# Pooled attention and two MoE layers on one core: down products without GpSimd, keys and values one unit ahead, weight units moved, tables in the weights' buffers

## Chip, cores and metric

One core of a Trainium2 chip runs the whole program in one launch. The metric is device time in microseconds (us). All matrix products are float32 in three passes: an operand is split into a rounded high part and the remainder, and high x high, high x low and low x high are added up in PSUM.

## What is computed

The reference, cut to what matters (q and k are drawn 8 times larger than here; the weights arrive as float64):

```python
B, H, S, D, pool = 8, 8, 576, 64, 8
k_p = k.reshape(B, H, S // pool, pool, D).mean(axis=3)      # the same for v_p
attn = softmax(q @ k_p.transpose(0, 1, 3, 2) / sqrt(D))
x = (attn @ v_p).transpose(0, 2, 1, 3).reshape(4608, 512)
h = x @ w_in                                                # 512 x 2048
y = (h * clip(h + 3, 0, 6) / 6) @ w_out                     # 2048 x 512
g = y @ w_gate                                              # 512 x 1536, w_val too
out = (g * sigmoid(g) * (y @ w_val)) @ w_out2               # 1536 x 512
```

## The kernel before

The program has four stretches.

**Start-up** computes the attention of the first 512 tokens. `load_first` stages its inputs in buffers that the weights will use later.

**The first stage** goes over nine blocks `j` of 512 tokens, and in each over 16 products `f` (`up`, 12 matmuls of 512 columns each, into one of three PSUM banks `h`). `act1` turns the result into `g` (ScalarE `t`, VectorE `g`, one of three `g32` buffers), and `store_g` writes it to `g_d` in HBM. Between the products stand, at two places per `f` (`attn_slot`), the steps of the attention for block `j + 1`. They are cut into units (a head pair and up to 256 queries); the table `when` (line 907) gives each step a unit offset and a place in the unit, and a sort over all units sets the order on every engine. `RK` sums keys on GpSimd, `K` transposes them and fills `kbd`; `S` scores, `X` exponents, `N`, `M` (GpSimd) normalise, `E` splits the tail, `T` transposes, `U` and `L` copy to `aT`, `V` multiplies with the values, `W` and `Y` write `x`. `R0` and `R1` sum values on GpSimd, `R` splits them into `vst` and `vtl`. Behind each product `prep_slot` does a step of a weight unit: the layers after the first product use sums and differences of weight quarters (Strassen-Winograd: 7 products in place of 8), and 26 units compute these tables and store them in HBM. A unit fetches (SyncE), rescales (ScalarE), joins the two halves of each float64 (VectorE, lines 127 and 130), sums (GpSimd, `sums_a` or `sums_b`), casts (ScalarE, 249), subtracts (VectorE, 252) and stores. 14 units (`PREP_A`) fall into the first stage. Block 8, the last, has no attention beside it. There `g` is stored from ScalarE's queue, four quarters of block 0's `g` (`gq`) are loaded at its start, and the seven tables `pw` of `w_out` at its end, when the first stage's pools close.

**The down stage** takes the nine blocks again, seven products each (`DN`; `down_b`, 48 matmuls of 256 columns in four chunks). The products' left sides are the quarters 11, 22, 12 or the sums S3 = 11 - 21, S2 = 22 - S3, S1 = S2 + 11, S4 = 12 - S2, computed in place in `gq`, each in two halves: S3 and S2 on VectorE, S1 and S4 on GpSimd (`sum_b`, line 803). `split_b` splits a chunk one product ahead into one of four `gb` buffers (ScalarE cast, line 135; VectorE subtraction, line 136). `evac_b` adds the results (line 841). The other 12 weight units run here, their sums on GpSimd.

**The second MoE** makes six passes over 768 tokens with seven-product schemes for all its products; its weight tables come through a ring of four tiles (`load_next`).

The order on each engine is the program's own (`manual_schedule`): an instruction that waits holds back all behind it on its engine, DMA issues on their queue too.

Of the kernel before, what the change touches and what calls it, by code (L numbers as in the profile page):

```python
# [23 lines left out]
def kernel(  # L24
# [45 lines left out]
    l1, l1_ps = ExitStack(), ExitStack()  # L70
    wu_p = l1.enter_context(tc.tile_pool(name="wu", bufs=F1))
    x_p = l1.enter_context(tc.tile_pool(name="x", bufs=2))
    t_p = l1.enter_context(tc.tile_pool(name="t", bufs=2))
# [9 lines left out]
    half = const.tile([P, 1], F32, name="half")  # L83

# [53 lines left out]
    class Weights:  # L138
# [14 lines left out]
        def convert(self):  # L153

            done, self.joined = self.joined, []
            parts = []
            for f, t in done:
                w = wu[f] = wu_p.tile([P, 2, KT, P], F32R, tag="wu", name="wu")
                w = w.rearrange("p a k f -> p a (k f)")
                nc.scalar.copy(out=w[:, 0], in_=f32(t))  # L160
                parts.append((w, t))
            scaled, self.scaled = self.scaled, []
            for f, s in scaled:
                t = t_p.tile([P, WC], I32, tag="w32", name="w32")
                join(s, t)
                self.joined.append((f, t))
            for w, t in parts:
                nc.vector.tensor_tensor(out=w[:, 1], in0=f32(t), in1=f32(w[:, 0]), op=ALU.subtract)
# [45 lines left out]
    def prep_step(u, step):  # L214
# [25 lines left out]
        elif step == 3:  # L240
            q = prep_t["f", u]
            if kind == "up":
                sums_a(nc.gpsimd, lambda n: q[:, A7[n]])
            else:
                sums_b(nc.gpsimd, lambda n: q[:, B7[n]])
# [18 lines left out]
    def x_tile(j):  # L264
        if j not in x_t:
            x_t[j] = x_p.tile([P, KT, 2, N], F32R, tag="x", name="x")
# [43 lines left out]
    def load_first(seg_n):  # L310
        def stage(name):
            return wu_p.tile([P, 2, POOL, D], F32, tag="wu", name=name)

        ks = [stage("ks") for _ in range(KT)]
        es_t.append(stage("es").rearrange("p h o d -> p (h o d)"))
        qs, vs, vt = ([stage(nm) for _ in range(KT // 2)] for nm in ("qs", "vs", "vt"))
# [258 lines left out]
    def act1(pool, ps):  # L575
        t = pool.tile([P, N], F32, tag="t", name="t")
        nc.scalar.activation(out=t, in_=ps, func=ACTF.Relu, bias=half, scale=1.0 / 6.0)  # L577
        g = pool.tile([P, N], F32, tag="g32", name="g32", bufs=3)
# [3 lines left out]
    def store_g(j, f, g, eng):  # L582
        eng.dma_start(out=g_d[j][:, :, f // NP1, f % NP1], in_=g.rearrange("p (r n) -> p r n", r=2))
# [204 lines left out]
    def load_pw(what):  # L788
        nc.sync.dma_start(
            out=f32(lb["pw", what]).rearrange("p f a n -> p (f a n)"),  # L790
            in_=s_w1[:, B7[what]].rearrange("p f a n -> p (f a n)"),
        )

    SLOT = {"11": 0, "S1": 0, "12": 1, "S4": 1, "21": 2, "S3": 2, "22": 3, "S2": 3}

    def sum_b(eng, j, what):
        a, b, op = {
            "S3": ("11", "21", ALU.subtract), "S2": ("22", "S3", ALU.subtract),
            "S1": ("S2", "11", ALU.add), "S4": ("12", "S2", ALU.subtract),
        }[what]  # L800
        for c in range(0, NP1, NP1 // 2):
            v = lambda x: gq[j, SLOT[x]][:, c:c + NP1 // 2]
            eng.tensor_tensor(out=v(what), in0=v(a), in1=v(b), op=op)  # L803

    def split_b(i, c):

        j, n = divmod(i, 7)
        if j < NB:
            t = gb[i, c] = lb["gb"].tile([P, 2, CB, MB], F32R, tag="gb", name="gb")
# [62 lines left out]
    for j in range(NB):  # L872
# [176 lines left out]
    right_b, left_b = ExitStack(), ExitStack()  # L1049
    with tc.manual_schedule():  # L1050
# [50 lines left out]
        pool, late = t_p, []  # L1101
        for j in range(NB):
            for f in range(F1):
                if j == NB - 1 and f == 0:
                    attn_ctx.close()
                    last_a = ExitStack()
                    lb["gq"] = right_b.enter_context(
                        tc.tile_pool(name="gq", bufs=1, side="right", reuse_waits="tile"))
                    pool = last_a.enter_context(
                        tc.tile_pool(name="tl", bufs=2, side="right", reuse_waits="tile"))  # L1110
                    for slot in (0, 3, 2, 1):
# [3 lines left out]
                if (j, f) == (NB - 1, F1 - 1):  # L1115
                    l1.close()
                    for nm, bufs in (("pw", 1), ("gb", 4)):
                        lb[nm] = left_b.enter_context(
                            tc.tile_pool(name=nm + "b", bufs=bufs, reuse_waits="tile"))
                    order = [what for _, _, what in DN]  # L1120
                    for n in (2, 3, 4, 1, 5, 0, 6):
                        what = order[n]
                        lb["pw", what] = lb["pw"].tile([P, NP1, 2, 2 * P], F32R, tag="pw" + what, name="pw")
                    for what in order:
                        load_pw(what)
                    for c in range(NCB):
                        split_b(0, c)
                attn_slot(j, 2 * f)
                g = act1(pool, hp)
                attn_slot(j, 2 * f + 1)  # L1130
                if j < NB - 1:
                    store_g(j, f, g, nc.sync)
                else:
                    for args in late:
                        store_g(*args, nc.scalar)
                    late = [(j, f, g)]
# [4 lines left out]
        for args in late:  # L1141
            store_g(*args, nc.scalar)
        last_a.close()
# [3 lines left out]

        for i in range(7 * NB):
            j, n = divmod(i, 7)
            if n == 0:  # L1150
                sum_b(nc.vector, j, "S3")
            down_b(i)
            if n == 1:
                sum_b(nc.vector, j, "S2")
            for c in range(NCB):
                split_b(i + 1, c)
            if n == 1:
                sum_b(nc.gpsimd, j, "S1")
                sum_b(nc.gpsimd, j, "S4")
            if 2 <= n <= 5:  # L1160
                load_g(j + 1, {2: 3, 3: 0, 4: 2, 5: 1}[n])
            evac_b(j, n)
            prep_slot(F1 * (NB - 1) + i)
            if j == NB - 1 and n >= 5:
                if n == 5:
# [4 lines left out]
                    l2["x"] = ctx.enter_context(  # L1170
                        tc.tile_pool(name="xc", bufs=1, side="right", reuse_waits="tile"))
                    l2["ys"] = ctx.enter_context(
                        tc.tile_pool(name="ys", bufs=1, side="right", reuse_waits="tile"))
                    load_y(0)
                for step in ((0, 1, 2), (3, 4, 5, 6))[n - 5]:
# [65 lines left out]
```

## Time and profile before

| what | us |
|---|---|
| median of 3 runs | 1958.4 (1957.16 to 1961.93) |
| profiled execution | 1956.7 |
| its span, first to last instruction | 1955.0 |
| TensorE busy in it | 1788.7 (91%) |
| VectorE busy | 1390.3 (71%) |
| ScalarE busy | 763.7 (39%) |
| GpSimd busy | 778.7 (40%) |

The profile names engines PE (TensorE), PEld (its weight loads), DVE (VectorE), ACT (ScalarE), POOL (GpSimd) and SP (SyncE). Busy time alone does not say what limits a stretch: an instruction that is held up inside counts as busy, and TensorE's busy time counts the same whether its clock is at the full or the lower level. PEclk is the mean granted clock as a share of the full one.

### The profile page before, as it was taken

How to read it: one execution, taken by the hardware profiler on the slowest of the kernel's cores; microseconds unless marked ns; L12 is line 12 of the kernel's file. 1: busy time of each engine (PE TensorE's matmuls, PEld its weight loads, DVE VectorE, ACT ScalarE, POOL GpSimd, SP SyncE). 2: the span in 40 equal slices, each digit the busy share in tenths (PEclk: the TensorE clock that was granted, in tenths of full speed). 3: DMA queues.
4: the chain of work that ended last, by engine and by line, in shares of the span. 5: the costliest groups of instructions: out<-in, count | busy, mean ns of one | idle time of the engine just before them, and what ended most of it. 6: DMA issues, size and time to landing. Idle time of an engine off the chain costs nothing.

```text
span 1955.0 us, 31356 instructions
## 1 busy us (share of the span) xinstructions
PE 1788.7 (91%) x11241; PEld 1669.5 (85%) x11241; DVE 1390.3 (71%) x2356; ACT 763.7 (39%) x1689; POOL 778.7 (40%) x886
## 2 busy tenths in 40 slices
PE   5998898888889988988889889999999999999999
PEld 3776686666767777888889889999999999999999
DVE  7766676666667368888888856766866767678566
ACT  5644444444434334544444432422422323224123
POOL 5336446365362024343433315335155053252360
PEclk8999999898989998999999899999999999999999
DMA  7745566465555785565555558797787887887876
GB/s 172 191 121 173 168 208 194 147 192 174 165 150 171 253 336 178 195 230 208 177 198 186 182 204 284 238 313 260 253 314 241 286 287 242 291 284 249 284 241 211
DMA packets 234828, 432.52 MB, mean 221 GB/s; under 512 B 86576, under 2 KB 168496, under 8 KB 218416
## 3 DMA queue, kind: packets, MB, share of 16 engines
q1 hardware_dynamic: 228176, 425.00, 65.6%
q10 hardware_dynamic: 6496, 5.51, 0.8%
q8 instruction: 89, 1.46, 0.3%
q14 instruction: 67, 0.55, 0.1%
HBM read 326.11 MB, written 104.33 MB: 220 GB/s over the span
## 4 chain that ended last, share of the span: by engine, by line
PE 45%; DVE 3%; issue 1%; DMA 1%; POOL 0%; ACT 0%; SPq 0%; ACTq 0%; DVEq 0%
PE b L648 41%; PE b L825 4%; DVE gb L136 2%; DVE gq L803 0%; DMA sdn<-s 0%; DVE s L252 0%; DMA ystg<-y 0%; POOL q L195 0%; DVE o L841 0%; DVE xc L136 0%; ACT gb L135 0%; DVE ystg L195 0%; POOL gq L803 0%; DVE q L127 0%; ACT xc L135 0%
## 5 line engine op out<-in xcount | busy, mean ns | idle before, releaser
L648 PE MATMUL b<-xc,wr 128*128 128x384 f32 x3024 | 527.8, 336 | 7.6 <-ACT xc L135 5.9
L648 PEld LDWEIGHTS b<-xc,wr 128*128 128x128 f32 x3024 | 525.5, 188 | 8.7 <-ACT xc L135 6.2
L566 PE MATMUL h<-x,wu 128*128 128x512 f32 x1728 | 456.5, 418 | 1.6 <-DVE g L579 1.6
L825 PE MATMUL b<-gb,pw 128*128 128x256 f32 x3024 | 393.1, 294 | 54.6 <-DVE gb L136 43.1
L825 PEld LDWEIGHTS b<-gb,pw 128*128 128x128 f32 x3024 | 385.2, 201 | 62.6 <-DVE gb L136 50.4
L566 PEld LDWEIGHTS h<-x,wu 128*128 128x128 f32 x1728 | 339.5, 202 | 73.2 <-DVE g L579 2.0
L657 DVE TENSOR_TENSOR c<-c,b 128x384 f32<-128x384 f32 x504 | 265.1, 552 | 178.0 <-PE b L648 154.3
L695 POOL TENSOR_TENSOR s<-s,c 128x384 f32<-128x384 f32 x144 | 143.1, 1019 | 411.0 <-ACT s L693 411.0
L136 DVE TENSOR_TENSOR gb<-gq,gb 128x512 fp32r<-128x512 f32 x252 | 247.5, 1020 | 72.8 <-ACT gb L135 72.2
L648 PE MATMUL b<-wr,gc 128*128 128x256 f32 x2268 | 273.1, 283 | 0.0
L648 PEld LDWEIGHTS b<-wr,gc 128*128 128x128 f32 x2268 | 272.9, 189 | 0.0
L135 ACT CAST gb<-gq 128x512 fp32r<-128x512 f32 x252 | 154.5, 621 | 221.7 <-PE b L825 199.0
L702 POOL TENSOR_TENSOR gf<-s,c 128x384 f32<-128x384 f32 x144 | 168.7, 1197 | 66.4 <-DVE c L657 65.9
L135 ACT CAST gc<-gf 128x768 fp32r<-128x768 f32 x126 | 105.7, 839 | 192.3 <-POOL gf L702 101.0
L803 POOL TENSOR_TENSOR gq<-gq 128x1024 f32<-128x1024 f32 x36 | 109.7, 3067 | 175.1 <-DVE gq L803 134.3
L501 POOL TENSOR_TENSOR e<-e,sm 96x288 f32<-96x288 f32 (+3 forms) x85 | 61.0, 717 | 252.5 <-DVE sm L497 195.8
L579 DVE SCALAR_TENSOR_TENSOR g<-t,h 128x512 f32<-128x512 f32 x144 | 98.2, 683 | 85.3 <-ACT t L577 64.3
L693 ACT ACTIVATE s<-c 128x384 f32<-128x384 f32 x144 | 73.4, 525 | 203.6 <-DVE c L657 202.4
L136 DVE TENSOR_TENSOR gc<-gf,gc 128x768 fp32r<-128x768 f32 x126 | 133.8, 1093 | 17.4 <-ACT gc L135 15.8
L577 ACT ACTIVATE t<-h,half 128x512 f32<-128x512 f32 x144 | 98.3, 682 | 41.8 <-PE h L566 33.3
L665 ACT COPY c<-b 128x384 f32<-128x384 f32 x72 | 33.9, 470 | 146.1 <-PE b L648 146.1
L458 PE MATMUL pss<-kbd,qT 128*128 128x144 f32 (+2 forms) x336 | 62.5, 305 | 22.5 <-ACT kbd L404 20.5
(105 smaller groups left out, 1758.1 us busy)
## 6 DMA issues: line engine op xcount, KB each, us to landing
wr<-sup SPq DMA_DIRECT2D x72, 1024.0 KB
wr<-sdn SPq DMA_DIRECT2D x84, 768.0 KB
wr<-sup SPq DMA_DIRECT2D x72, 768.0 KB
gq<-g SPq DMA_DIRECT2D x36, 1024.0 KB
g<-g SPq DMA_DIRECT2D x128, 256.0 KB
sup<-s SPq DMA_DIRECT2D x12, 1792.0 KB
wstg<-in_moe_w_out_dram SPq DMA_DIRECT2D x56, 256.0 KB
sw<-s SPq DMA_DIRECT2D x8, 1792.0 KB
```

The source lines that it names most:

```text
L135: nc.scalar.copy(out=hi, in_=src)
L136: lo_engine.tensor_tensor(out=lo, in0=src, in1=f32(hi), op=ALU.subtract)
L566: nc.tensor.matmul(out=ps, lhsT=w(kt, wh), rhs=x(kt, xh), start=first and n == 0, stop=last and n == 3 * len(kts) - 1,)
L577: nc.scalar.activation(out=t, in_=ps, func=ACTF.Relu, bias=half, scale=1.0 / 6.0)
L579: nc.vector.scalar_tensor_tensor(out=g, in0=t, scalar=1.0, in1=ps, op0=ALU.min, op1=ALU.mult)
L648: nc.tensor.matmul(out=ps, lhsT=w(wh), rhs=x(xh), start=first and n == 0, stop=last and n == 2)
L657: add = lambda dst, a, b: nc.vector.tensor_tensor(out=dst, in0=a, in1=b, op=ALU.add)
L693: nc.scalar.activation(out=g[q], in_=c[q], func=ACTF.Sigmoid)
L695: nc.gpsimd.tensor_tensor(out=g[q], in0=g[q], in1=c[q], op=ALU.mult)
L702: nc.gpsimd.tensor_tensor(out=gf[p][:, GP[TURN[q]], f], in0=g[q], in1=c[q], op=ALU.mult)
L803: eng.tensor_tensor(out=v(what), in0=v(a), in1=v(b), op=op)
L825: nc.tensor.matmul(out=ps[:, d], lhsT=w[:, CB * c + k, wh, P * d:P * (d + 1)], rhs=g[:, gh, k], start=what == place and (c, d, k, m) == (0 ...
```

## The change

- **Down stage.** S1 and S4 run on VectorE, in halves laid out over products 1 to 5. S3 is gone from this stage: `act1` computes it on GpSimd in the first stage, in place in `g`, before the store, for the products `f` < 8. The remaining weight units are summed on VectorE. The quarters of the next block are loaded behind products 3, 4 and 5 in place of 2 to 5.
- **Attention order.** `RK`, `K`, `R0`, `R1`, `R` move one unit ahead; `V`, `W`, `Y` move eight places later in their unit.
- **Weight units.** 20 in the first stage, one every 5.5 products in place of 8; six in the down stage, one every nine.
- **Buffers.** The weights of four `f` share one 4096-column buffer of four; `load_first` takes slices of the same. The tables `pw` go into a buffer of their own (the first), the two `x` buffers and the weights' four, each as block 8's last product has read it. `g` is stored from SyncE's queue in all blocks, and has three `t` buffers.
- **Second MoE.** The ring lies elsewhere, and its first load is issued two products earlier.

```diff
-    PREP_A = 14
+    PREP_A = 20
     for u in range(len(preps)):
-        first = 8 * u if u < PREP_A else F1 * (NB - 1) + 9 * (u - PREP_A) // 2
+        first = 11 * u // 2 if u < PREP_A else F1 * (NB - 1) + 9 * (u - PREP_A)
...
-            q = prep_t["f", u]
+            q, eng = prep_t["f", u], nc.gpsimd if u < PREP_A else nc.vector
             if kind == "up":
-                sums_a(nc.gpsimd, lambda n: q[:, A7[n]])
+                sums_a(eng, lambda n: q[:, A7[n]])
...
+        if f < NP1:
+            nc.gpsimd.tensor_tensor(out=g[:, MB:], in0=g[:, :MB], in1=g[:, MB:], op=ALU.subtract)
         return g
...
-        "RK": (-1, 14), "K": (0, 11), "P": (-1, 4), "S": (1, 0), "X": (1, 1), "N": (1, 5),
-        "M": (1, 5), "E": (1, 12), "T": (2, 16), "U": (2, 17), "L": (2, 18), "V": (3, 6),
-        "W": (3, 7), "Y": (3, 12), "R0": (1, 21), "R1": (2, 15), "R": (2, 19),
+        "RK": (-2, 14), "K": (-1, 11), "P": (-1, 4), "S": (1, 0), "X": (1, 1), "N": (1, 5),
+        "M": (1, 5), "E": (1, 12), "T": (2, 16), "U": (2, 17), "L": (2, 18), "V": (3, 14),
+        "W": (3, 15), "Y": (3, 20), "R0": (0, 21), "R1": (1, 15), "R": (1, 19),
...
+                    load_g(0, 0)
+                    load_pw(0, lambda name: lb["px"].tile([P, BIG], F32R, tag="px", name=name))
+                    load_pw(1, big_x)
+                    for slot in (3, 2, 1):
                         load_g(0, slot)
...
+                store_g(j, f, g)
...
+                if j == NB - 1:
+                    if f % 4 == 3:
+                        load_pw(2 + f // 4, big_w)
+                    if 10 <= f < 10 + NCB:
+                        split_b(0, f - 10)
...
+        sums_at = {1: (("S2", 0), ("S2", 1)), 2: ((), ("S1", 0)), 3: (("S1", 1), ()),
+                   4: ((), ("S4", 0)), 5: (("S4", 1), ())}
...
-            if n == 0:
-                sum_b(nc.vector, j, "S3")
             down_b(i)
-            if n == 1:
-                sum_b(nc.vector, j, "S2")
             for c in range(NCB):
+                if c % (NCB // 2) == 0 and sums_at.get(n, ((), ()))[c // (NCB // 2)]:
+                    sum_b(j, *sums_at[n][c // (NCB // 2)])
                 split_b(i + 1, c)
-            if n == 1:
-                sum_b(nc.gpsimd, j, "S1")
-                sum_b(nc.gpsimd, j, "S4")
-            if 2 <= n <= 5:
-                load_g(j + 1, {2: 3, 3: 0, 4: 2, 5: 1}[n])
+            for slot in {3: (0,), 4: (2,), 5: (3, 1)}.get(n, ()):
+                load_g(j + 1, slot)
```

Three places of the engines' order. The first is VectorE in the down stage, from the last `g` to the adds of products 2 and 5 of block 0 (`gb<-gq,gb` is the subtraction of a split, `gq<-gq` half a sum, `o` an evacuation add). Before:

```order
L803 TENSOR_TENSOR gq<-gq 128x1024 x2
L136 TENSOR_TENSOR gb<-gq,gb 128x512 x4
L803 TENSOR_TENSOR gq<-gq 128x1024 x2
L136 TENSOR_TENSOR gb<-gq,gb 128x512 x8
L841 TENSOR_TENSOR o_7806<-o_7668,b 128x512
```

After:

```order
L145 TENSOR_TENSOR gb<-gq,gb 128x512 x4
L816 TENSOR_TENSOR gq<-gq 128x1024
L145 TENSOR_TENSOR gb<-gq,gb 128x512 x2
L816 TENSOR_TENSOR gq<-gq 128x1024
L145 TENSOR_TENSOR gb<-gq,gb 128x512 x4
L816 TENSOR_TENSOR gq<-gq 128x1024
L145 TENSOR_TENSOR gb<-gq,gb 128x512 x2
L854 TENSOR_TENSOR o_7971<-o_7838,b 128x512
L816 TENSOR_TENSOR gq<-gq 128x1024
L145 TENSOR_TENSOR gb<-gq,gb 128x512 x6
```

The half sums no longer come in pairs, and those of S1 (the third and fourth) stand on this engine. GpSimd's list, which had four half sums in each block, has nothing between block 8 of the first stage and the second MoE.

The second is TensorE at the head of the last batch in the first stage (`psk<-ident,kp` transposes keys, `pss<-kbd` scores; `kbd_116` before and `kbd_119` after is the first head pair's). Before:

```order
L546 MATMUL psv<-aT,vst_122 128x192
L547 MATMUL psv<-aTt,vtl_126 128x192
L393 MATMUL psk<-ident,kp 128x72
L518 MATMUL pst<-ident,e 128x128 x2
L522 MATMUL pst<-ident,et_131 96x128 x2
L458 MATMUL pss<-kbd_116,qT 64x144
L566 MATMUL h<-x,wu 128x512 x12
```

After:

```order
L406 MATMUL psk<-ident,kp 128x72
L557 MATMUL psv<-aT,vst_125 128x192
L558 MATMUL psv<-aT,vst_125 128x192
L559 MATMUL psv<-aT,vst_125 128x192
L560 MATMUL psv<-aTt,vtl_129 128x192
L579 MATMUL h<-x,wu 128x512 x12
L531 MATMUL pst<-ident,e 128x128 x2
L535 MATMUL pst<-ident,et_134 96x128 x2
L471 MATMUL pss<-kbd_119,qT 64x144
```

Before, the first pair's scores follow its key transpose with no product `h` between; after, the transpose shown is already the second pair's, and the first pair's stands a product further up. Over the 28 head pairs behind start-up, 0 to 2 products stood between transpose and scores, and now 2 to 4.

The third is SyncE's DMA queue at the start of block 8 (`sup` is a weight unit's store, `g` a store of `act1`'s result). Before, with block 8's stores of `g` on ScalarE's queue:

```order
L583 DMA g_97<-g_7252 256x1x256
L254 DMA sup_105<-s_7235 128x3584
L786 DMA gq<-g_90 128x2048 x4
L789 DMA pw<-sw_99 128x4096 x7
L109 DMA wstg<-in_moe_w_gate_dram 128x2x256 x4
```

After:

```order
L266 DMA sup_114<-s_7408 128x3584
L801 DMA gq<-g_93 128x2048
L807 DMA pw<-sw_102 128x4096 x2
L801 DMA gq<-g_93 128x2048 x3
L598 DMA g_101<-g_7464 256x1x256
L598 DMA g_101<-g_7483 256x1x256
L598 DMA g_101<-g_7502 256x1x256
L598 DMA g_101<-g_7521 256x1x256
L807 DMA pw<-sw_102 128x4096
```

Two of the seven tables now stand among the four quarters at the block's start, and the block's stores follow on the same queue, with one table behind every fourth.

## Rows read from the trace of the kernel before

**Rows 1.** Busy us (and instructions) by engine and stage; granted clock, DMA share

```profile
core 0: us, PE busy (x) PEld busy (x) DVE busy (x) ACT busy (x) POOL busy (x), PEclk, DMA share, GB/s
51.00:648.00 597.00, 522.96 (x2596) 427.59 (x2596) 403.93 (x971) 270.22 (x794) 279.04 (x456) 0.93 0.58 171
648.00:696.00 48.00, 46.42 (x206) 38.12 (x205) 14.66 (x21) 15.05 (x22) 0.00 (x0) 1.00 0.73 260
696.00:1144.00 448.00, 393.38 (x3027) 385.20 (x3025) 371.41 (x393) 200.71 (x318) 162.01 (x84) 0.94 0.59 208
1144.00:1955.00 811.00, 799.07 (x5292) 797.94 (x5292) 564.59 (x877) 247.13 (x419) 311.83 (x288) 1.00 0.77 266
```

**Rows 2.** Instruction groups, whole run: busy us, mean ns, idle us before, releasers

```profile
L825 PE MATMUL b<-gb,pw 128*128 128x256 f32 x3024 | 393.1, 294 | 54.6 <-DVE gb L136 43.1 <-ACT gb L135 10.4 <-DMA pw<-sw 0.6
...
L841 DVE TENSOR_TENSOR o<-o,b 128x512 f32<-128x512 f32 x45 | 30.6, 679 | 0.3
```

**Rows 3.** Timeline of ScalarE, undisturbed down stage: start us, us, idle before

```profile
788.31 0.62 ACT L135 CAST gb<-gq 128x512 fp32r<-128x512 f32 x1 [0.82 <-PE b L825]
789.75 0.62 ACT L135 CAST gb<-gq 128x512 fp32r<-128x512 f32 x1 [0.82 <-PE b L825]
```

**Rows 4.** Timeline of the down stage while GpSimd computes S1 and S4

```profile
760.50 5.99 POOL L803 TENSOR_TENSOR gq<-gq 128x1024 f32<-128x1024 f32 x2 [15.07 <-DVE gq L803]
761.42 9.03 DVE L136 TENSOR_TENSOR gb<-gq,gb 128x512 fp32r<-128x512 f32 x4
...
764.32 7.88 PE L825 MATMUL b<-gb,pw 128*128 128x256 f32 x48 [2.53 <-DVE gb L136]
```

**Rows 5.** Instructions of the tile gq: duration ns min/median/max, first and last start

```profile
L136 DVE TENSOR_TENSOR gb<-gq,gb x252: 674/692/2910, 695.2 to 1138.9; 128x512 fp32r<-128x512 f32 x126
...
L803 DVE TENSOR_TENSOR gq<-gq x36: 1208/1217/1760, 698.2 to 1107.2; 128x1024 f32<-128x1024 f32 x36
```

**Rows 6.** Groups on VectorE and GpSimd, 51 to 648 us (blocks 0 to 7)

```profile
L579 DVE SCALAR_TENSOR_TENSOR g<-t,h 128x512 f32<-128x512 f32 x126 | 86.0, 682 | 52.7 <-ACT t L577 48.7 <-DMA g<-g 2.8 <-ACT kbd L404 0.3
...
L252 DVE TENSOR_TENSOR s<-q,s 128x1792 fp32r<-128x1792 f32 x13 | 26.4, 2031 | 0.0
...
L130 DVE SCALAR_TENSOR_TENSOR q<-wstg,q 128x512 int32<-128x512 int32 x28 | 22.8, 815 | 1.0
...
L195 POOL TENSOR_TENSOR q<-q 128x256 f32<-128x256 f32 x32 | 22.7, 732 | 2.8 <-DVE q L130 2.2
```

**Rows 7.** What TensorE waited for, 51 to 696 us: total us, times, longest

```profile
PE pss L458 <- ACT kbd L404: 18.7, 7, 4.3
PE psv L545 <- DVE aT L538: 16.2, 24, 1.9
PE psv L547 <- DVE vtl L429: 14.2, 9, 2.4
PE psv L544 <- ACT vst L135: 10.6, 12, 2.4
```

**Rows 8.** Timeline around one wait for keys in the first stage

```profile
466.18 1.69 ACT L249 CAST s<-q 128x1792 fp32r<-128x1792 f32 x1 [2.20 <-POOL q L190]
...
468.49 0.85 PE L458 MATMUL pss<-kbd,qT 128*128 128x144 f32 x2 [3.65 <-ACT kbd L404]
```

**Rows 9.** Block 8: DMA issues, DMA rate 698 to 724 us, timelines

```profile
gq<-g SPq DMA_DIRECT2D x36, 1024.0 KB
...
sup<-s SPq DMA_DIRECT2D x12, 1792.0 KB
...
pw<-sw SPq DMA_DIRECT2D x7, 2048.0 KB
...
698.00:724.00 26.00, 23.68 (x191) 22.86 (x190) 23.89 (x22) 10.78 (x18) 11.56 (x4) 1.00 1.01 422
...
654.93 13.47 SPq L786 DMA_DIRECT2D gq<-g  x4
...
668.19 0.69 DVE L579 SCALAR_TENSOR_TENSOR g<-t,h 128x512 f32<-128x512 f32 x1 [7.49 <-DMA g<-g]
...
668.93 27.54 PE L566 MATMUL h<-x,wu 128*128 128x512 f32 x120 [1.58 <-DVE g L579]
```

More of the change, by code (lines that the diff above doesn't have):

```diff
@@ L311, in stage @@
         def stage(name):
[L312 to L316, printed above, removed]
+            t = f32(big_w(name)).rearrange("p (i h o d) -> p i h o d", i=4, h=2, o=POOL)
+            return [t[:, i] for i in range(4)]
+        ks, qv, ev = (stage(nm) for nm in ("ks", "qv", "ev"))
+        qs, vs, vt = qv[:2], qv[2:], ev[2:]
+        es_t.append(ev[0].rearrange("p h o d -> p (h o d)"))
         for t in vt:
@@ L786, in load_g, with load_pw, sum_b @@
             nc.sync.dma_start(out=t, in_=g_d[j][:, r, c])
[L788 to L796, printed above, removed]
+    def load_pw(n, tile_of):
+        what = DN[n][2]
+        t = tile_of("pw")
+        lb["pw", what] = t.rearrange("p (f a n) -> p f a n", f=NP1, a=2)
+        nc.sync.dma_start(out=f32(t), in_=s_w1[:, B7[what]].rearrange("p f a n -> p (f a n)"))
+    SLOT = {"11": 0, "S1": 0, "12": 1, "S4": 1, "S3": 2, "22": 3, "S2": 3}
+    def sum_b(j, what, half):
         a, b, op = {
-            "S3": ("11", "21", ALU.subtract), "S2": ("22", "S3", ALU.subtract),
-            "S1": ("S2", "11", ALU.add), "S4": ("12", "S2", ALU.subtract),
+            "S2": ("22", "S3", ALU.subtract), "S1": ("S2", "11", ALU.add), "S4": ("12", "S2", ALU.subtract),
         }[what]
-        for c in range(0, NP1, NP1 // 2):
-            v = lambda x: gq[j, SLOT[x]][:, c:c + NP1 // 2]
-            eng.tensor_tensor(out=v(what), in0=v(a), in1=v(b), op=op)
+        v = lambda x: gq[j, SLOT[x]][:, NP1 // 2 * half:NP1 // 2 * (half + 1)]
+        nc.vector.tensor_tensor(out=v(what), in0=v(a), in1=v(b), op=op)
     def split_b(i, c):
@@ L1099, in load_next @@
                 sent[0] += 1
-        pool, late = t_p, []
         for j in range(NB):
             for f in range(F1):
-                if j == NB - 1 and f == 0:
+                if (j, f) == (NB - 1, 0):
                     attn_ctx.close()
[L1106 to L1111, printed above, removed]
+                    for nm in ("gq", "px"):
+                        lb[nm] = right_b.enter_context(
+                            tc.tile_pool(name=nm, bufs=1, side="right", reuse_waits="tile"))
+                    load_g(0, 0)
+                    load_pw(0, lambda name: lb["px"].tile([P, BIG], F32R, tag="px", name=name))
+                    load_pw(1, big_x)
+                    for slot in (3, 2, 1):
                         load_g(0, slot)
@@ L1114 @@
                 up(hp, wu[f], x_tile(j))
[L1115 to L1127, printed above, removed]
                 attn_slot(j, 2 * f)
-                g = act1(pool, hp)
+                g = act1(f, hp)
                 attn_slot(j, 2 * f + 1)
[L1131 to L1136, printed above, removed]
+                store_g(j, f, g)
                 if j == 0:
@@ L1140 @@
                     prep_slot(F1 * (j - 1) + f)
-        for args in late:
-            store_g(*args, nc.scalar)
-        last_a.close()
+                if j == NB - 1:
[3 more added lines that the diff above has]
+                        split_b(0, f - 10)
+        load_pw(6, big_x)
+        l1.close()
         l1_ps.close()
@@ L1169 @@
                     assert not prep_at
[L1170 to L1173, printed above, removed]
+                    for nm, to, bufs in (("xc", "x", 1), ("ys", "ys", 1), ("wr", "ring", 4)):
+                        l2[to] = ctx.enter_context(
+                            tc.tile_pool(name=nm, bufs=bufs, side="right", reuse_waits="tile"))
                     load_y(0)
+                    load_next()
                 for step in ((0, 1, 2), (3, 4, 5, 6))[n - 5]:
                     x_step(0, step, nc.vector, nc.vector)
+        load_next()
         left_b.close()
[L1178 removed]
+        for nm, bufs in (("gf", 1), ("gc", 6), ("t", 1), ("o", 1)):
             l2[nm] = ctx.enter_context(tc.tile_pool(name=nm + "2", bufs=bufs, reuse_waits="tile"))
[L1180 to L1181 removed]
         for p in range(NG):
```

50 lines of the change are left out of this document (28 added, 22 removed).

## The prediction

> **What bounds the kernel now.** I read the busy time by stage first. The program runs four stretches after 51 us of start-up: blocks 0 to 7 of the first MoE's up products with the attention between them, block 8 of them alone, the down products, and the second MoE [rows 1]. In the last one TensorE is busy for 799 of 811 us at a granted clock of 1.00; the change leaves its loops alone, so I leave it at 811 us. The other stretches hold the slack. A mean clock of 0.94 over the down stage's 448 us is 0.06 x 448 = 27 us given away to the lower of the two clock levels, and the matmul group adds 54.6 us of idle, 43.1 of it behind VectorE's `gb` [rows 1, 2]. So the down matmuls themselves need 448 - 27 - 55 = 366 us. A second reading agrees: where nothing disturbs, ScalarE starts a cast each 1.44 us, once per chunk of 12 matmuls [rows 3], and 252 chunks x 1.44 = 363 us. Blocks 0 to 7 split in the same way: 597 us, of which TensorE idles 597 - 523 = 74 and loses 0.07 x 597 = 42 to the clock, which leaves 481 of work [rows 1].
>
> Why VectorE is late in the down stage stands in the timeline: while GpSimd computes two weight-sum tables of the activations (S1 and S4), four splits of VectorE take 9.03 us where the median one takes 0.692, and TensorE waits 2.53 us there [rows 4, 5]. The longest split took 2910 ns [rows 5], about one GpSimd instruction. VectorE's 371 busy us in that stage [rows 1] are thus mostly blocked time.
>
> **The down stage.** What goes is every GpSimd instruction: S1, S4 and the sums of the weight units. VectorE's load per block of 7 products, at undisturbed durations: 28 splits x 0.692 = 19.4; six half sums (S2, S1, S4) x 1.217 = 7.3; five evacuation adds x 0.679 = 3.4 [rows 2, 5]. Six weight units remain for nine blocks; each has one split of 2.03, two joins of two instructions at no more than 0.82, and four sums of 128x256 that now run on VectorE [rows 6]. No row has that sum on VectorE; it lies between half of a 128x512 split and the whole, 0.35 to 0.69 us, and I take 0.69: 2.03 + 3.3 + 2.8 = 8.1 per unit, 5.4 per block. Total 35.5 us against 28 x 1.44 = 40.3 us of TensorE. VectorE fits, at 88%. It must also fit locally. The last split of a product is due at its start, so between it and the first split of the next product VectorE has about one product (5.8 us) less the two splits and the cast's delay, some 3.5 us. The worst queue there is an evacuation add, a weight step and a half sum, 0.68 + 2.03 + 1.22 = 3.9 us, so TensorE waits some 0.5 us in a handful of the 63 products. I add 3 us for this, 2 for clock, 2 for the first product: 365 + 7 = **372 us, 76 less**. The ends are 366 and 390 (a stall of 0.4 us in every product).
>
> Nothing is late in the place of GpSimd: tables of the next block are requested with at least 1.5 products (9 us) of lead; one is 1024 KB, 2.5 us at 422 GB/s [rows 9].
>
> **Blocks 0 to 7.** Keys and values move one unit ahead. The waits for `kbd`, `vtl` and `vst` are 18.7 + 14.2 + 10.6 = 43.5 of the 74 us [rows 7]. The order shows the transposed keys now two products or more before their scores, in place of none or one. One unit is about 6 us and none of these waits was longer than 4.3 [rows 7] (one of 3.65 us behind ScalarE, itself blocked 2.20 us by GpSimd's sums, is typical [rows 8]), so I count all of them away. The waits on `aT`, 16.2 us in 24 pieces, stay: 26 of 96 units still have no product between transpose and use, 27 before. That leaves 30.
>
> Added there: 64 subtractions S3 on GpSimd, 128x256, 0.732 each as for the same shape [rows 6], 47 us; six weight units more, whose four sums are 4 x 0.732 x 6 = 18 us on GpSimd and (2.03 + 3.3) x 6 = 32 us on VectorE. GpSimd goes from 279 to 344 us, VectorE from 404 to 436, in a stretch that I expect at 540. This is where I doubt most. The subtraction waits for `g`, and queued behind it on GpSimd are key and value sums, the scaling of `e`, and the sums for ScalarE's weight cast; ScalarE and VectorE wait for these in order. Below it costs 0, above it gives all 43.5 us back with their clock; I take 12, nearer the lower end since GpSimd stays idle a third of the time. Idle is then 42. Clock loss was 42 us for 74 of idle, 0.57 for each; the waits that stay are short (0.7 us apiece), so I take 0.4, 17 us. 481 + 42 + 17 = **540 us, 57 less**. Ends: 523 (30 idle x 1.4) and 597.
>
> What S3 does to VectorE: `g` takes 682 ns on average, equal to its undisturbed time, although GpSimd is busy 47% of that stretch; it reads one operand from PSUM [rows 1, 6]. The Trainium skill (SBUF — State Buffer, Who interferes with whom) says that GpSimd and a VectorE instruction with two SBUF inputs exclude each other for a whole instruction, but not one with a single SBUF input. The rows agree on both sides. Were `g` blocked like a split, 64 x 0.73 = 47 us more would lie on VectorE.
>
> **Block 8.** The stores of `g` move from ScalarE's queue to SyncE's, behind 8192 KB of loads (four `gq`, two tables), that stand behind a 1792 KB store. Before, four `gq` loads began at 654.93, and even with its own queue a store held VectorE for 7.49 and TensorE for 1.58 us [rows 9]. Now 10.2 MB at 422 GB/s is 24.2 us: the first store follows at 679.1 and takes 0.6 us, the next `g` 0.7; landing, which no row shows, I set at 1 us, between nothing and the 4 us that the upper end below allows. TensorE goes on near 681.4. Three `g32` buffers and three PSUM banks let TensorE run six products ahead, so the seventh, due at 668.93 - 1.58 = 667.35, waits 14 us in place of 1.6. At 0.3 to 0.4 us of clock for each of the 12.4 us that are new, 4 us more, block 8 costs **16 us more**, 64. The later tables (2048 KB per four products, 5 us of 11) cost nothing. Ends: 0 if stores pass the loads, 20 if landing is slow. The Trainium skill (DMA: Bandwidth & Descriptors, Queues, rings and completion order) says that a DMA engine serves queues in turn, packet by packet, and one queue in ring order. By that rule the old stores shared the engines and the new ones stand behind all 10.2 MB; the sum above would be without the 16 us if the rule failed. Where the down stage starts, its tables 5 and 6 arrive within 10 us and are needed 29 us in, so their loading hides.
>
> Start-up: the staging tiles are slices of larger buffers, and the first matmuls wait for the same things; 0. Start of the second MoE: its `xc` casts follow the same evacuations; 0, within 3 us.
>
> **Sum.** -57 + 16 - 76 = -117. The profiled execution took 1956.7 us (the median is 1958.4, 0.1% above): 1956.7 - 117 = **1840 us**.
>
> **The rivals.** *First MoE gains nothing:* GpSimd, ScalarE and VectorE, which pass each unit on in order, set the pace; 436 us of VectorE plus its waits is not far below 540. Against: their idle is mostly for want of work. 1840 + 57 = 1897. *Block 8 does not stall*, as another queue order would give: 1824, and 1805 if the twelve us of new waits with their clock also stay away. *VectorE bounds the down stage,* some 0.5 us per product with clock: 35 us more, 1875; for it the 88%, against it the four chunks of slack. *Slower than before:* the store of `g` now waits for GpSimd, and a `g32` buffer returns only after it. A buffer has three products, some 12.6 us at 540/128 each; when GpSimd's backlog exceeds about 8 us, VectorE and then TensorE stop in every product with a subtraction. It would take 64 x 1.9 us to bring 1840 to 1964; GpSimd's idle third speaks against it. *The change does not do what it says:* the order shows no GpSimd instruction between block 8 and the second MoE, which excludes that.
>
> **How the numbers follow.** Forecast 0.52 (its own range 1824 to 1862); first MoE without gain 0.15; block 8 without stall 0.17; VectorE-bound 0.12; slower 0.04. Range 1800 to 1900: it takes in all cases but the last, and the bounds of both stages where they do not all fall on one side. A measurement here can tell 0.3%, 6 us, from no change: faster 0.95, same 0.02, slower 0.03.
>
> **What would show it.** Down stage near 372 us with a clock of 0.98 or more, no `gb` wait above 1 us, splits at 0.69 at most; no `kbd`, `vtl`, `vst` waits over 5 us in sum; in block 8 one wait for `g` of 10 us or more behind DMA. The prediction is wrong if blocks 0 to 7 still take 590, if splits stay slow without GpSimd, or if block 8 runs through.

## The result, and the profile after

The changed kernel takes **1985.3 us** (median of 4 runs, 1984.8 to 1987.1) against 1959.3 for the kernel before in the same comparison: ratio 1.0134, 95% interval 1.0116 to 1.0151. It is slower by 26 us; the forecast was 1840, and its range ended at 1900. Busy us by stage (columns as in [rows 1]; start-up ends at 53, block 7 at 755):

```profile
53.00:755.00 702.00, 548.87 (x2611) 447.65 (x2610) 446.17 (x1001) 285.52 (x816) 345.26 (x541) 0.89 0.56 170
755.00:818.00 63.00, 47.35 (x197) 38.60 (x196) 15.20 (x21) 13.48 (x22) 5.83 (x8) 0.86 0.86 316
818.00:1181.00 363.00, 362.39 (x3024) 361.90 (x3022) 282.77 (x402) 184.88 (x298) 0.00 (x0) 1.00 0.53 188
1181.00:1985.00 804.00, 793.26 (x5292) 792.18 (x5292) 564.50 (x877) 247.45 (x419) 310.71 (x288) 0.99 0.78 269
```

In [rows 1] the cut before block 8 lay at 648; with it at the end of block 7, as here, the kernel before reads:

```profile
53.00:651.00 598.00, 523.96 (x2606) 428.59 (x2605) 403.11 (x969) 272.09 (x795) 278.60 (x455) 0.93 0.57 170
651.00:696.00 45.00, 43.42 (x192) 35.60 (x191) 13.55 (x19) 12.51 (x19) 0.00 (x0) 1.00 0.78 277
```

In the profiled executions blocks 0 to 7 went from 598 to 702 us (+104), block 8 from 45 to 63 (+18), the down stage from 448 to 363 (-85), the second MoE from 811 to 804. Both kernels are cut at 53 us, but the first product `h` starts at 50.8 before and at 53.3 after: start-up is 2.5 us longer, and from its own start the stage takes 102 us more. The down stage answers to [rows 2, 5]: its TensorE group and the instructions of tile `gb`, durations min/median/max in ns:

```profile
L838 PE MATMUL b<-gb,pw 128*128 128x256 f32 x3024 | 362.6, 283 | 0.0
```

```profile
L145 DVE TENSOR_TENSOR gb<-gq,gb x252: 681/690/694, 805.8 to 1175.4; 128x512 fp32r<-128x512 f32 x126
```

No idle is left, and the slowest split takes 694 ns where it took 2910. In blocks 0 to 7 the waits of [rows 7] are gone and two others are there: the matmuls of `V` wait for VectorE's `x`, the step `Y` of the unit before, and the key transposes wait for GpSimd's key sums `kp` (us, times, longest us):

```profile
PE psv L557 <- DVE x L572: 118.4, 54, 6.8
PE psk L406 <- POOL kp L382: 31.0, 16, 4.4
```

The engines behind TensorE show more. ScalarE's `E` waits for GpSimd's `M` in 85 of the 96 units; in the kernel before, in 63. Its waits, before and after:

```profile
ACT et L508 <- POOL e L501: 68.2, 63, 4.5
```

```profile
ACT et L521 <- POOL e L514: 144.9, 85, 5.0
```

One unit in the timeline after, other engines' rows left out:

```profile
299.94 0.30 DVE L477 TENSOR_REDUCE mx<-pss 128x2 f32<-128x144 f32 x1
...
300.28 0.31 DVE L498 TENSOR_TENSOR e<-pss,mx 128x144 f32<-128x144 f32 x1
...
300.62 0.32 ACT L501 ACTIVATE e<-e 128x144 f32<-128x144 f32 x1 [1.31 <-DVE e L498]
300.98 0.30 DVE L508 TENSOR_REDUCE sm<-e 128x2 f32<-128x144 f32 x1 [0.39 <-ACT e L501]
...
301.31 0.17 DVE L509 TENSOR_SCALAR sm<-sm 128x2 f32<-128x2 f32 x1
301.52 0.17 DVE L510 RECIPROCAL sm<-sm 128x2 f32<-128x2 f32 x1
...
301.85 0.43 POOL L514 TENSOR_TENSOR e<-e,sm 128x144 f32<-128x144 f32 x1 [3.41 <-DVE sm L510]
...
302.31 0.22 ACT L521 CAST et<-e 128x32 fp32r<-128x32 f32 x1 [1.37 <-POOL e L514]
302.44 0.26 ACT L568 CAST x<-psv 128x128 fp32r<-128x128 f32 x1
302.56 0.45 DVE L524 TENSOR_TENSOR et<-e,et 128x16 f32<-128x16 f32 x1 [0.88 <-ACT et L521]
302.59 0.69 ACT L590 ACTIVATE t<-h,half 128x512 f32<-128x512 f32 x1
```

From `mx` to the second `et` these are nine instructions of one unit on three engines, each of which needs the one before it. VectorE and ScalarE do nothing for another unit in between, except ScalarE's `x` after the first `et`: ScalarE runs 0.32 us between 300.62 and 302.31, and what stands behind (`x`, `t`) waits with it.

Why nothing stands between: `attn_slot` (line 1095) runs the sorted steps up to the next `S`, `V` or `T`, and a product of the first layer, or its `t` and `g`, comes between two such stretches. Before, a unit's period was S X N M | V W K Y E | T U L (sums of keys and values left out); with V, W and Y eight places later, past E at 12, it is **S X N M K E | V W | T U L Y**.

### The profile page after: what moved, and what is told of

Same layout as the page of the kernel before. It is cut to its first block, busy times and chain, and to the rows that moved or that the text cites. A ratio compares the mean times of both kernels' runs of the same rounds, so it can differ in the third digit from the quotient of the medians.

```text
span 1985.4 us, 31395 instructions
## 1 busy us (share of the span) xinstructions
PE 1781.0 (90%) x11241; PEld 1663.1 (84%) x11241; DVE 1346.6 (68%) x2398; ACT 761.5 (38%) x1689; POOL 690.7 (35%) x898
## 4 chain that ended last, share of the span: by engine, by line
PE 69%; DVE 9%; DMA 6%; POOL 6%; ACT 6%; issue 4%; SPq 1%; POOLq 0%; DVEq 0%; ACTq 0%
PE b L663 40%; PE b L838 18%; PE h L579 9%; POOL e L514 2%; DMA g<-g 1%; DVE g L592 1%; DMA q_in<-in_q_dram 1%; ACT t L590 1%; DVE x L572 1%; DVE mx L477 1%; POOL vts L425 1%; DMA qv<-in_q_dram 1%; DVE sm L508 1%; POOL k_in L382 1%; ACT s L261 1%
## 5 line engine op out<-in xcount | busy, mean ns | idle before, releaser
L579 PE MATMUL h<-x,wu 128*128 128x512 f32 x1728 | 477.6, 433 | 19.0 <-DVE g L592 16.9
L579 PEld LDWEIGHTS h<-x,wu 128*128 128x128 f32 x1728 | 355.2, 212 | 96.0 <-DVE g L592 17.9
L838 PEld LDWEIGHTS b<-gb,pw 128*128 128x128 f32 x3024 | 362.3, 191 | 0.4 <-DVE gb L145 0.2
L838 PE MATMUL b<-gb,pw 128*128 128x256 f32 x3024 | 362.6, 283 | 0.0
L663 PE MATMUL b<-wr,gc 128*128 128x256 f32 x2268 | 265.6, 279 | 0.0
L663 PEld LDWEIGHTS b<-wr,gc 128*128 128x128 f32 x2268 | 265.4, 188 | 0.0
L145 DVE TENSOR_TENSOR gb<-gq,gb 128x512 fp32r<-128x512 f32 x252 | 168.6, 689 | 72.9 <-ACT gb L144 71.6
L557 PE MATMUL psv<-aT,vst 128*128 128x256 f32 (+3 forms) x96 | 34.8, 362 | 123.7 <-DVE x L572 118.4
L557 PEld LDWEIGHTS psv<-aT,vst 128*128 128x128 f32 x96 | 20.9, 218 | 138.7 <-issue 61.4
L501 ACT ACTIVATE e<-e 96x288 f32<-96x288 f32 (+3 forms) x76 | 31.4, 413 | 191.4 <-DVE e L498 191.4
```

The lines of the kernel that those rows point to most:

```text
L145: lo_engine.tensor_tensor(out=lo, in0=src, in1=f32(hi), op=ALU.subtract)
L579: nc.tensor.matmul(out=ps, lhsT=w(kt, wh), rhs=x(kt, xh), start=first and n == 0, stop=last and n == 3 * len(kts) - 1,)
L663: nc.tensor.matmul(out=ps, lhsT=w(wh), rhs=x(xh), start=first and n == 0, stop=last and n == 2)
L838: nc.tensor.matmul(out=ps[:, d], lhsT=w[:, CB * c + k, wh, P * d:P * (d + 1)], rhs=g[:, gh, k], start=what == place and (c, d, k, m) == (0 ...
```

## The experiments

Theory A: the order costs, as `E` now stands in one stretch with `M`. B: the order costs, as `V`, `W`, `Y` come late (one PSUM buffer `psv`, freed only by `Y`). C: GpSimd's added load (S3, six weight units) costs. The expectations of e1, e2, e4 and e6 use these letters otherwise: their theory A is B here (in e6 the order as a whole), and their theory B is its opposite (in e1, C). Each was cut out or put in alone, except that some runs also move the stores of block 8, which touches only that block. The table has blocks 0 to 7, cut as above, and ScalarE's wait of `E` for `M` in them. A stage is read from one profiled execution, and executions of the kernel before ran from 1953.4 to 1964.1 us in one comparison, so a difference of a few us between two rows is not clear of noise.

| run | blocks 0 to 7, us | wait, us | median, us |
|---|---|---|---|
| before / after | 598 / 702 | 68 / 145 | 1959 / 1985 |
| e6: before, new table | 674 | 150 | 2037 |
| e9: before, keys and values ahead | 598 | 80 | 1962 |
| e12: before, E late | 586 | 3 | 1946 |
| e19: e12, twenty units | 620 | 8 | 1960 |
| e1: after, Y early | 705 | 153 | 1989 |
| e4: after, two halves of psv | 699 | 145 | 1985 |
| e2: after, V, W, Y early | 643 | 87 | 1930 |
| e8: e2, E beside M | 711 | 160 | 1996 |
| e3: after, old table | 647 | 86 | 1934 |
| e7: after, E late | 630 | 8 | 1915 |
| e10: e7, S3 on VectorE | 629 | 8 | 1910 |
| e11: e7, 14 units | 641 | 3 | 1927 |
| e13: e10 and e11 | 640 | 3 | 1922 |
| e14: e7 without S3 | 613 | 7 | 1900 |
| e15: e7, V, W, Y early | 633 | 9 | 1912 |
| e16: e7, old table but E | 641 | 14 | 1922 |
| e17: e16, S3 on VectorE | 641 | 10 | 1921 |
| e18: e10, 14 units, new spacing | 611 | 8 | 1893 |

### Is it the table, and which step of it?

**The table alone** in the kernel before:

```diff
-        "RK": (-1, 14), "K": (0, 11), ... "V": (3, 6), "W": (3, 7), "Y": (3, 12), "R0": (1, 21), "R1": (2, 15), "R": (2, 19),
+        "RK": (-2, 14), "K": (-1, 11), ... "V": (3, 14), "W": (3, 15), "Y": (3, 20), "R0": (0, 21), "R1": (1, 15), "R": (1, 19),
```

> The kernel before with the new table of attention steps alone: no S3 and no more weight units on GpSimd in the first stage, down stage as before. Theory A: blocks 0 to 7 lose here what they lost in the change, 60 to 100 us, time 2015 to 2060. Theory B: they gain what the moved keys and values give, time 1920 to 1965.

The ratio is 1.0396 (1.033 to 1.0462), with 76 us more in blocks 0 to 7 with nothing added to any engine. The order costs, and C is not the main cause.

**V, W, Y back**, and **Y alone back**, in the changed kernel:

```diff
-"V": (3, 14), "W": (3, 15), "Y": (3, 20)
+"V": (3, 6), "W": (3, 7), "Y": (3, 12)
```

> The changed kernel with V, W and Y back at places 6, 7 and 12 of their unit as in the kernel before; keys and values stay one unit ahead. Theory A: the waits for x fall to the 5 us of before, the waits for kbd, vst and vtl stay away, blocks 0 to 7 take some 560 us, and the time is 1850 to 1900. Theory B: blocks 0 to 7 stay near 690 us and the time above 1960.

```diff
-"Y": (3, 20)
+"Y": (3, 15)
```

> The changed kernel with one number altered: step Y (VectorE's low half of x, which frees the one PSUM buffer of the value product) stands at place 15 of its unit in place of 20, ahead of the next unit's transpose and copies. Theory A (TensorE's 118 us of waits for x come from Y standing behind other units' work on VectorE): these waits fall below 50 us and the time to about 1910 to 1940. Theory B (GpSimd's added work, S3 and six weight units, makes VectorE and ScalarE late whatever the place of Y): the waits only change their name, and the time stays at 1970 to 1990.

The first gives 0.9848 (0.9777 to 0.9919), with 643 us in blocks 0 to 7, between its two expectations. The second gives 1.0151 (1.0087 to 1.0215), with nothing gained. With `Y` straight behind `W` the wait on `x` falls to 26.2 us, and others take its place:

```profile
PE psk L406 <- POOL kp L382: 46.3, 15, 6.0
PE psv L558 <- DVE aT L551: 38.7, 41, 3.1
PE psv L557 <- DVE x L572: 26.2, 10, 5.0
PE psv L557 <- ACT aT L544: 18.6, 13, 2.9
```

So the wait that adds up to most in the profile was not the cause. **Two halves of the bank** for `psv` in turn:

```diff
-            pool, tag = ps_y, "y2"
+            i = n_ps["v"] = 1 - n_ps["v"]
+            return n_ps["vt"][:, i, :shape[1]]
```

> The changed kernel with two halves of the one PSUM bank used in turn for the value product, so that V no longer needs the previous unit's Y. Theory A: the waits of V for x fall from 118 us to under 15, and the time to 1860 to 1910. Theory B: other waits take their place (psk for kp, which were 31 us, and aT), and the time stays above 1950.

The ratio is 1.0127, with the wait where it was:

```profile
PE psv L560 <- DVE x L575: 121.7, 55, 6.8
```

`V` still starts only when the other half has been read: all 55 waits end with the `Y` of the unit directly before. So this run didn't remove the wait and decides nothing; the run before it does.

**E apart from M**, with V, W, Y late, and the converse, **E beside M** with V, W, Y early (on e2):

```diff
-"E": (1, 12)
+"E": (1, 21)
```

> The changed kernel with one entry of the table altered: E (split of the tail, which waits for GpSimd's scaling M) goes from (1, 12) to (1, 21), so that it no longer stands in the same stretch of the order as S, X, N and M, with no first-layer product between M and E, but after T, U, L, R and Y. V, W and Y stay late. Theory A (what costs is that E stands behind M in one stretch, so that ScalarE and VectorE, in order, wait for GpSimd's M each time): most of the 55 us that the early V, W, Y gave back come here too, 1920 to 1945 us, ScalarE's wait of the E step for GpSimd falls from 145 us (85 times) to under 60, and the waits of V on Y shrink. Theory B (what costs is that V, W and Y themselves come late, close before T and U, in a burst): 1975 to 1995 us, with the waits of V unchanged.

```diff
-"E": (1, 12), "V": (3, 6), "W": (3, 7)
+"E": (1, 6), "V": (3, 7), "W": (3, 8)
```

> The converse: the changed kernel with V, W, Y early (3, 7), (3, 8), (3, 12), as in the run that gave 1930 us but for one place: E at (1, 6), before V instead of after W, so that it stands in one stretch with M. Theory A: the loss comes back, 1965 to 1995 us, with ScalarE waiting over 120 us for GpSimd's M. Theory B: V, W, Y are early, so it stays at 1920 to 1940 us.

Ratios 0.978 (0.9747 to 0.9812) and 1.0196 (1.0172 to 1.022). One entry takes 72 us from blocks 0 to 7; putting E beside M costs 68 there with V, W, Y early. A holds both ways, B falls. ScalarE's wait with E late, and its order at the same place:

```profile
ACT et L521 <- POOL e L514: 7.7, 9, 2.2
```

```profile
300.06 0.44 ACT L501 ACTIVATE e<-e 128x288 f32<-128x288 f32 x1 [4.22 <-DVE e L498]
300.41 0.45 ACT L417 ACTIVATE kbd<-psk 64x72 f32<-64x72 f32 x2
300.88 0.69 ACT L590 ACTIVATE t<-h,half 128x512 f32<-128x512 f32 x1
301.47 0.36 ACT L568 CAST x<-psv 128x256 fp32r<-128x256 f32 x1
302.01 0.37 ACT L544 CAST aT<-pst 128x256 fp32r<-128x256 f32 x1 [0.18 <-PE pst L535]
302.27 0.37 ACT L545 CAST aTt<-pst 96x256 fp32r<-96x256 f32 x1
302.54 0.25 ACT L521 CAST et<-e 128x64 fp32r<-128x64 f32 x1
```

Between the exponents and `et` ScalarE now does the work of other units, and GpSimd has `M` done by then.

**V, W, Y early and E late** (with the stores of block 8 on ScalarE's queue, below):

> The changed kernel with E late and V, W, Y early (keys and values ahead, S3 on GpSimd, 20 units), and the stores of block 8 on ScalarE's queue. If the late V, W, Y still cost (the waits of V on Y, 38 us), blocks 0 to 7 fall from 630 us to 595 to 615 and the run to 1870 to 1892; if their place matters no more once E stands apart from M, 622 to 638 and 1900 to 1918 (block 8 gives 5).

Blocks 0 to 7 take 633 us against 630 in e7: once E stands apart, the place of V, W, Y is worth nothing that this can tell.

### What are keys and values ahead worth?

Before with `RK`, `K`, `R0`, `R1`, `R` alone moved, and after with the table of before:

> The kernel before with RK, K, R0, R1, R alone moved one unit ahead; V, W, Y, E and all else as before. By the forecast's count of waits (18.7 for kbd, 14.2 for vtl, 10.6 for vst): 1910 to 1925 us. Rival (the waits of the products only change their names, since VectorE, ScalarE and GpSimd pass their time round among themselves): 1950 to 1965. The third possibility, that keys and values ahead cost: over 1970.

> The changed kernel with the whole table of before (keys and values prepared as late as before, V, W, Y early): what is left of the change in blocks 0 to 7 is GpSimd's S3 in eight slots a block and the twenty weight units. If keys and values one unit ahead give back the waits that I counted (43 us), it is 1960 to 1980 us, 40 above the run with V, W, Y early (1930), and the waits for kbd, vst and vtl of before are back. Rival: preparing ahead gives nothing here (what came off these waits is waited for elsewhere) and it is 1920 to 1940. Below 1915: preparing ahead costs.

Ratios 1.0011 (0.9992 to 1.003) and 0.9879 (0.9853 to 0.9906), both as the rival said. In the first, the waits for `kbd`, `vtl` and `vst` are gone, and blocks 0 to 7 take 598 us as before. TensorE waits for other things:

```profile
PE psv L545 <- DVE aT L538: 36.1, 43, 4.3
PE psv L544 <- ACT aT L531: 30.6, 18, 5.4
```

`aT` had 16.2 [rows 7] and 4.1 us. The waits changed their name. After with the old table but for E late:

> The changed kernel with the table of before but for E late: against the kernel before with E late (586 us in blocks 0 to 7) it differs only by S3 on GpSimd and the weight units. If these two are the load that costs, blocks 0 to 7 stay at 620 to 640 us and the run at 1900 to 1925; if keys and values ahead or the late V, W, Y cost, they fall to 590 to 610 and the run to 1875 to 1895.

Blocks 0 to 7 take 641 us, 8 more than with keys and values ahead (633 in e15). With S3 on VectorE the same step gives 12 (641 in e17, 629 in e10). So with more load, and E apart, moving them ahead gains some 10 us. In this stage it differs from e19 (620, below) in S3 and the new buffers alone; they cost 21 us, most of it S3 (17, e14 below).

### What does GpSimd's new load cost?

**S3 on VectorE** (with the stores of block 8 on ScalarE's queue, one product late), and the same on the old table but for E:

```diff
-            nc.gpsimd.tensor_tensor(out=g[:, MB:], ...
+            nc.vector.tensor_tensor(out=g[:, MB:], ...
```

> Two parts on top of the changed kernel with E late (1915 us; blocks 0 to 7 took 630 us there, block 8 stood 16 us for its seventh product). First, S3 of the first layer on VectorE instead of GpSimd: if GpSimd's added load is what still holds blocks 0 to 7 above the 597 us of before, they fall to 600 to 615; if VectorE is as tight as GpSimd, they stay at 625 to 645. Second, in block 8 alone the stores of g go out on ScalarE's queue, one product later, and no longer behind the 10.2 MB of loads on SP's: if that queue is the cause of the wait of 16 us, it falls under 6; if the transfers themselves are (the memory is busy with the loads, whichever queue asks), it stays over 10. In all 1870 to 1890 us by the first two, 1905 to 1930 by the rivals.

> The run before with S3 on VectorE, and the stores of block 8 on ScalarE's queue. If GpSimd is the tight engine with this table, blocks 0 to 7 fall by 10 to 30 us against the run before; if, as with the new table, it makes no difference who subtracts, within 4 us. Block 8 is 5 us shorter in either case.

Blocks 0 to 7 take 629 us against 630, and 641 against 641. An S3 takes 489 ns (median) on VectorE in e10 and 732 on GpSimd in e7, but the means are 685 and 812, and the longest takes 2.5 us on either engine. **No S3 at all:**

> The changed kernel with E late, without the subtraction S3 in the first layer (eight of 16 slots of each block; the third product of the down stage then takes block 21 of g instead of S3, so the output is another). Blocks 0 to 7 took 630 us. If S3 is what costs, by its 64 x 0.73 us and by the wait for g ahead of it on GpSimd, they fall to 585 to 605 and the run to 1870 to 1890; if it is the table or the six units, they stay at 620 to 635 and the run at 1905 to 1920.

Blocks 0 to 7 take 613 us, between the two expectations: S3 costs 17 us on either engine, and is not the whole. **Weight units**, 14 in the first stage at the old spacing, on e7 and on e10:

```diff
-    PREP_A = 20
+    PREP_A = 14
-        first = 11 * u // 2 if u < PREP_A ...
+        first = 8 * u if u < PREP_A ...
```

> The changed kernel with E late, and 14 weight units in blocks 0 to 7 instead of 20, spaced as before; S3 stays on GpSimd. If the six units cost their share of GpSimd's load, blocks 0 to 7 fall from 630 us to 610 to 622; if S3 in eight slots of each block is the whole of the 32 us, they stay at 626 to 634. The six units then run in block 8 and the down stage, on VectorE and ScalarE there: 0 to 20 us longer than 362 us. In all 1895 to 1925.

> The changed kernel with E late, S3 on VectorE, 14 weight units in the first stage, and the stores of block 8 on ScalarE's queue. If the parts add up: blocks 0 to 7 at 590 to 605 us, block 8 at 48 to 52, down stage 362 to 380: 1855 to 1880 in all. If the six units take in the down stage what they free in the first: no better than the run with 20 units, S3 on VectorE and the same stores.

Blocks 0 to 7 take 641 and 640 us, 11 *more* with fewer units. Of the expectations only e13's "no better" came, and not for its reason: the down stage took the six units for some 4 us, and the first stage gave nothing back. **14 units at the new spacing**, and **20 units at the new spacing in the kernel before with E late**:

> The changed kernel with E late, S3 on VectorE and the stores of block 8 on ScalarE's queue (1910 us; blocks 0 to 7 629), with 14 weight units in the first stage at the new spacing (every 5.5 slots, so they end after five blocks). If the six units are what is left of the loss, blocks 0 to 7 fall to 600 to 615 us, all of it in blocks 5 to 7; if it is the spacing that sets what collides, blocks 1 to 4 stay and 5 to 7 change by less than 8. The six units add 0 to 15 us to the down stage.

> The kernel before with E late (1946 us; blocks 0 to 7 586) and twenty weight units in the first stage, every 5.5 slots, as in the change, S3 still in the down stage. If the six units cost the open 27 us there: blocks 0 to 7 at 605 to 620, and the down stage, rid of them, 0 to 15 us shorter. If not, 582 to 592, and the open part is in the changed kernel's other edits of the first stage (its buffers).

The first differs from e13 in the spacing alone: 611 us against 640. From e10 (629) it differs by 18 us, in blocks 6 and 7 alone, where most of the six units were; so six units cost 18 us at one spacing, 3 each. The second has 620 against 586: 34 us for the six units and the closer spacing together; 18 of it come back in the down stage, whose matmul group (busy and idle before it) goes from 391.7 + 56.0 to 386.4 + 43.4 us. The same step, from 14 units at 8 to 20 at 5.5, takes 11 us off in the changed kernel (e13 to e10). What the spacing is worth thus depends on what else stands in the order, in sign too. A spacing of 8 puts the units at the same two products of every 16-product block, 5.5 does not; that this sets what they collide with is argued, not shown.

**E late in the kernel before:**

> The kernel before with E alone moved, from (1, 12) to (1, 21). ScalarE waited 68 us there for GpSimd's M, with only V's stretch between M and E. If that wait held blocks 0 to 7 back in the kernel before too, they fall by 20 to 40 us: 1920 to 1940. If it was hidden behind other waits (as the 43 us for keys and values were): 1950 to 1962.

The ratio is 0.9936 (0.9921 to 0.9951), with 12 us less in blocks 0 to 7, between the two expectations. Of the 68 us that ScalarE waited there, most was hidden.

### Block 8

The wait for the seventh product after, in the timeline: the store that waits on SyncE's queue, VectorE behind it, TensorE:

```profile
764.85 23.98 SPq L598 DMA_DIRECT2D g<-g  x4
...
786.79 2.04 DVE L592 SCALAR_TENSOR_TENSOR g<-t,h 128x512 f32<-128x512 f32 x3 [21.62 <-DMA g<-g]
```

```profile
787.54 30.42 PE L579 MATMUL h<-x,wu 128*128 128x512 f32 x120 [15.65 <-DVE g L592]
```

In e10 the stores go out on ScalarE's queue, one product later, and TensorE stops three times:

```profile
703.14 5.04 PE L579 MATMUL h<-x,wu 128*128 128x512 f32 x12 [4.58 <-DVE g L592]
710.95 18.27 PE L579 MATMUL h<-x,wu 128*128 128x512 f32 x72 [2.76 <-DVE g L592]
730.84 8.48 PE L579 MATMUL h<-x,wu 128*128 128x512 f32 x36 [1.62 <-DVE g L592]
```

It waits 9.0 us in place of 16.3 in e7, between the two expectations, and block 8 is five shorter. Some 7 us came from the place in the queue; the rest stays, and VectorE still waits for stores. Whether the loads that run beside them or the later issue cause it was not separated.

### The best version

e18 (E late, S3 on VectorE, 14 units at 5.5, stores of block 8 on ScalarE's queue) takes 1893.2 us, ratio **0.9663 (0.9646 to 0.968)** to the kernel before:

```profile
53.00:664.00 611.00, 515.63 (x2612) 423.50 (x2612) 436.77 (x1038) 266.12 (x799) 286.56 (x453) 0.94 0.58 170
664.00:720.00 56.00, 47.53 (x193) 38.34 (x192) 16.52 (x28) 13.13 (x20) 0.00 (x0) 0.91 0.90 338
720.00:1085.00 365.00, 362.98 (x3015) 361.38 (x3014) 310.95 (x455) 197.36 (x313) 0.00 (x0) 1.00 0.64 230
```

The down stage takes the six units back for some 4 us (its matmuls run to 1086.6, just behind the cut), though VectorE there goes from 283 to 311 us busy.

## Why the prediction was wrong

**The down stage was right:** -85 for -76. The clock was 1.00, no wait was left and splits took 0.69 us: the 7 us that I added for stalls and clock did not come. A 128x256 sum on VectorE takes 0.422 us (24 of them), inside 0.35 to 0.69; I took the upper end. GpSimd's absence cured VectorE: with GpSimd idle, the longest split fell from 2910 to 694 ns. The Trainium skill (SBUF — State Buffer, Who interferes with whom) has the two exclude each other for VectorE instructions with two SBUF inputs; these durations agree. One reading was too strong: VectorE's 371 busy us were not *"mostly blocked time"*. The splits were busy for 247.5 us, and 252 of them at 0.692 are 174, so that some 73 us were blocked.

**Block 8 came out as forecast, but for half of the reason:** one wait of 15.7 us for 14, and +18 for +16. The sum put all of the new wait down to the place in the queue; on another queue 9.0 us of waits stay (e10), so the fit of the size is partly luck. **Second MoE:** 0 within 3 was forecast, -7 measured. It was not followed up; every run built on the changed kernel has it (803 to 805 us from the end of the down stage, against 811 to 813 in those built on the kernel before).

**Blocks 0 to 7 were wrong:** -57 forecast, +104 measured. In the terms of the sum, TensorE's idle is 702 - 549 = 153 us for 42, and the clock takes 0.11 x 702 = 77 us for 17. Three steps failed.

1. *The move of V, W and Y had no term at all.* Alone it is worth 59 us (e2 to after). The late place itself costs nothing that the runs can tell (e15); but the move passed E, and so put E into one stretch with M. Taking E out of that stretch gives 72 us (after to e7), putting it in costs 68 (e2 to e8), and the whole table costs 76 in the kernel before (e6). I had read the new order on TensorE, where keys come earlier, and not on ScalarE, where `et` came to stand behind the exponents with nothing in between.
2. *"I count all of them away"*: the 43.5 us of waits for `kbd`, `vtl` and `vst` went, and the time did not follow (0 in e9, 4 in e2 against e3, some 10 with E late). TensorE's wait names which of several late things came last, not what each is worth. (The keys had stood 0 to 2 products ahead of their scores, not "none or one".) The rival "first MoE gains nothing" said that the other engines pass each unit on in order; that was the mechanism, priced at 0 where the order could make it worse.
3. *"I take 12"* for GpSimd's new load, 17 us with its clock, with 0 and 43.5 (61 with clock) as ends: everything of the change but the table costs 49 us (before to e3), so the upper end was nearer. S3 measured 17 of it, the six units 18, and with the closer spacing 34 in the kernel before.

The runs lead from before to after in three steps: all but the table +49 (598 to 647, e3), keys and values ahead -4 (643, e2), V, W and Y late +59 (702). Put together from e12 instead: 586 + 34 (e19) + 17 (e14) - 8 (e15, e16) = 629; e7 has 630, and E beside M makes it 702. That this agrees to 1 us is luck: each price was taken in other surroundings, and by the same prices 14 units at a spacing of 8 would take 586 + 17 - 8 = 595, where e11 has 641. Why that spacing costs so much more in the changed kernel stays open.

The rival "slower" was priced for another mechanism (`g32` buffers held by GpSimd); S3 on VectorE, where no `g32` waits for GpSimd, gained 1 us (e10). Of the signs named for a wrong prediction, "blocks 0 to 7 still take 590" is the one that came, and by far more.

## What to carry to other kernels

Where a sorted table sets the order, read the new order on every in-order engine, between each pair of steps that hand a result to another engine and back, and count what stands between them: a step moved past another can bring producer and consumer together though neither was meant to move. A wait of the busiest engine can be worth nothing when other things are late behind it, so test one such wait alone before counting a sum of them. Where fill-in work falls in a loop can cost more than the work itself, and which spacing is better can change with the rest of the order; try another spacing before fewer pieces.

## What was not expected

Fewer weight units at a spacing of 8 products made the stage 11 us longer, and 14 units at 5.5 beat 14 at 8 by 29 us with equal work. S3 cost the same 17 us on VectorE (0.685 us each on average) and on GpSimd (0.812). Two halves of one PSUM bank, used in turn, still followed each other: the wait was 121.7 us against 118.4; whether the chip asks for that or the program's own bookkeeping of the tile was not separated.
